# A fused adaLN attention and MLP kernel: the turn of x's blocks 1 to 3 moved from TensorE to VectorE and DRAM, with new instruction orders

## The chip, the cores and the metric

One core of a Trainium2 chip runs the whole kernel. The metric is the device time of one execution in microseconds; less is better. Inputs and outputs are fp32 in DRAM.

The engines are called TensorE (PE in the profile, PEld for its weight loads), VectorE (DVE), ScalarE (ACT), GpSimd (POOL) and SyncE (SP). SP issues nearly all DMAs here.

## The reference

One block of a transformer with adaptive layer norms: linear attention, then an MLP with SiLU. S = 2048 tokens, D = 576, H = 32 heads of 18, F = 4608.

```
mod = silu(c) @ w_mod                      # (1,576) @ (576, 6*576)
sa, ca, ga, sb, cb, gb = six rows of mod
h = layernorm(x) * (1 + ca) + sa
q, k, v = heads of h @ wqkv                # (2048,576) @ (576,1728)
pq, pk = phi(q), phi(k)                    # t+1 where t > 0, else exp(t); + 1e-6
kv = sum over tokens of pk^T v             # per head, 18 x 18
z  = sum over tokens of pk
x = x + ga * (((pq @ kv) / (pq . z)) @ wo)
h = layernorm(x) * (1 + cb) + sb
out = x + gb * (silu(h @ w1) @ w2)
```

## The kernel before

**Number format.** Products run in fp32r, a format that TensorE takes in one pass. Each fp32 operand is split in a high part (a cast on ACT, `split_h` L205, `w_hi` L309) and a low part (a subtraction on VectorE or GpSimd, `sub_hi` L121, `w_lo` L315 and L317). A product is hi·hi + hi·lo + lo·hi. The contraction over D = 576 goes in four chunks of 128 (KC = 4) and a tail of 64, whose high and low part share the 128 rows. So one output bank takes 14 matmuls (`x_passes` L222): per chunk hi·hi, hi·lo, lo·hi, in chunk order 0 to 4.

**Tokens.** 16 tiles of 128 (NT), in 4 blocks of 512 (NB). `hT[tb]` holds a block's normalised, modulated x with D on the partitions, in high and low parts.

**Stages.** First the head (to about 37 us): the modulation columns of the first layer norm come from w_mod, the tiles of block 0 are turned by TensorE (`turn_tiles` L387), and k and v of tiles 0 and 1 are computed. Then a loop over the tiles t = 0 to 15 (from L643): k projection, v projection, the products kv of tile t−1 (`kv_mm`), and q projections of the first eight tiles (`q_proj`, q0 and q1 at t = 1). wq for the q projections is loaded into rooms of `acc` and split at t = 1 (`split_w`). At t = 4 and t = 7 two thirds of w_mod's rest are multiplied by silu(c) (`mod_piece` L508), of which the first piece is loaded (`raw`, L266) and scaled (`tmod`, L517) much earlier by the written order. After the loop come the attention output, the second layer norm and the MLP, whose h streams through DRAM and whose main units (L1324 and on) run from 372 us to the end. From about 400 us on code and order stay as they are.

**The turn of blocks 1 to 3 in before.** At t = 0, 4, 8 `load_x` (L258) loads the four tiles of the next block into `xt` (a pool with four places). At i = t mod 4 = 1 the statistics, and the normalised rows in place: tiles 1 and 3 on ACT (L191), 0 and 2 on VectorE (L193). At i = 2 and 3 `turn` (L633) takes one chunk after the other: four TensorE transposes of 128x128 into the PSUM bank psT (`transpose_chunk` L212 to L214), then on ACT the modulation out of PSUM (L199) and the cast to the high part (L205), then on VectorE the low part. That makes 3 blocks x 5 chunks x 4 = 60 transposes. The next block is first used by the k projection at the next t = 4, 8, 12.

**Order.** ORDERS holds for each engine a list of instruction numbers; `arrange` ties each instruction behind the one before it in the list. In before TensorE's list changes two places only, since the program's own order holds there (`manual_schedule`); VectorE, ACT, GpSimd and SP have long lists up to about 400 us.

**Rooms.** A tile of a pool waits until the users of the tile whose place it takes are done. `xt_133` and `xt_135` (136 and 138 in before) are x's tiles 2 and 3; the third and fourth tile of block 1 take their places.

Of the kernel before, what the change touches and what calls it, by code (L numbers as in the profile page):

```python
# [16 lines left out]
P = 128  # L17
# [5 lines left out]
def kernel(ctx: ExitStack, tc, A_x, A_wqkv, A_wo, B_x, B_w1, B_w2, c, w_mod, out):  # L23
# [28 lines left out]
    def f32(ap):  # L52
# [4 lines left out]
            0-106 114 107-109 115 110-113 116-2586  # L57
        """,
        "DVE": """
            0 3 2 1 4 6-7 11 8 12-13 9-10 14-16 18 17 5 19-22 30 23-24 28-29 25-27 43 31 44 33-34 36 35 37-38 32 39  # L60
            41 40 42 45-47 50 48-49 62-63 51-53 57 84 64 55 58 65 59 86 66 85 87 60 56 80 67 88 81 83 68 82 69 71 70
            72 122 73-74 61 89 54 75 78 76 90 77 79 123 91 124 92-93 96-97 125 98 94 126-127 100 99 95 101 103-104
            107 105 108 106 109 111 102 132-133 135 110 134 136 138-139 137 140-144 112 145 148 113 146 149 147 114
            117 115 118 116 119-121 128-129 131 150-151 225 223 130 226 224 222 152-155 157-158 156 159 162 176 160
            177-178 161 179-181 163 165 228 227 166-167 164 169-170 168 171-173 193-197 199 198 200 202 201 203-205
            174 209 206-207 210 208 175 182 185 183 186 188 187 184 189-190 192 191 211-213 216 214 217 215 218 220
            219 221 229 232 230 233 231 234-237 240 238-239 241-243 246 244 247 245 248-249 252 250-251 253-256 258
            257 259 263 260-262 266 268 267 270 269 271 264-265 272-273 275-277 274 281 279 282 278 280 283-284 288
            285 289 286 295-296 290 306 303 302 291 307 292 314 293 315 294 297 323 304 298-299 324 308 331 287 300
            309 301 310-311 305 312 316 332 340 313 317-319 341 320-321 325 351 322 326-329 352 362 330 333-336 338  # L70
            363 337 339 344 370 345-347 342-343 349 348 353 371 380 354-359 350 360 381 361 398 364-369 399 416
            372-375 377 376 378 417 424 385 382 384 379 387-388 391-392 394 425 402 386 389 403 390 404-407 393 383
# [568 lines left out]
    with tc.manual_schedule(engines={mybir.EngineType.PE}):  # L641
        for t in range(NT):
# [4 lines left out]
            if t > 1:  # L647
                k_proj(t)
# [944 lines left out]
```

## Time and profile before

| what | us |
|---|---|
| median of three timed runs (1137.52 to 1138.51) | 1137.76 |
| profiled execution, span from its first to its last instruction | 1136.9 |
| time around the span (the median less the span) | 0.9 |
| TensorE busy in the span | 1126.8 |
| VectorE busy | 971.0 |
| GpSimd busy | 649.3 |
| ACT busy | 538.7 |

In a row of the timeline the first number is the start, the second the time from the first start to the last end of so many equal instructions. TensorE's matmuls overlap, so the spacing of starts tells what one costs. In a row of the windows stand the length, the busy times of PE, PEld, DVE, ACT and POOL with their counts, then the granted clock, the share of the DMA engines' time and GB/s. A row of the waits names who waited at which line, for whom, the sum in us, the count and the longest.

### The profile page before, as it was taken

How to read it: one execution, taken by the hardware profiler on the slowest of the kernel's cores; microseconds unless marked ns; L12 is line 12 of the kernel's file. 1: busy time of each engine (PE TensorE's matmuls, PEld its weight loads, DVE VectorE, ACT ScalarE, POOL GpSimd, SP SyncE). 2: the span in 40 equal slices, each digit the busy share in tenths (PEclk: the TensorE clock that was granted, in tenths of full speed). 3: DMA queues.
4: the chain of work that ended last, by engine and by line, in shares of the span. 5: the costliest groups of instructions: out<-in, count | busy, mean ns of one | idle time of the engine just before them, and what ended most of it. 6: DMA issues, size and time to landing. Idle time of an engine off the chain costs nothing.

```text
span 1136.9 us, 19287 instructions
## 1 busy us (share of the span) xinstructions
PE 1126.8 (99%) x7033; PEld 1040.8 (92%) x7033; DVE 971.0 (85%) x1543; ACT 538.7 (47%) x1112; POOL 649.3 (57%) x743
## 2 busy tenths in 40 slices
PE   8999999999999999999999999999999999999998
PEld 7999999999998899999999999999989999999998
DVE  6866744686878899999999999999999999999996
ACT  5643442547556544445445444444444444444441
POOL 1100000374714777767775776677667767776786
PEclk9999999999999999999999999999999999999999
DMA  9621100223359877976978869779778697697684
GB/s 281 199 84 31 44 7 1 71 84 116 137 198 354 340 274 256 348 278 257 361 261 315 314 250 356 273 255 364 261 277 331 265 344 281 258 346 274 256 310 156
DMA packets 58813, 269.03 MB, mean 237 GB/s; under 512 B 5724, under 2 KB 21856, under 8 KB 35680
## 3 DMA queue, kind: packets, MB, share of 16 engines
q1 hardware_dynamic: 58708, 267.80, 64.4%
q8 instruction: 56, 0.92, 0.3%
q14 instruction: 37, 0.30, 0.1%
q10 hardware_dynamic: 12, 0.00, 0.0%
HBM read 250.12 MB, written 16.78 MB: 235 GB/s over the span
## 4 chain that ended last, share of the span: by engine, by line
PE 94%; DMA 3%; DVE 1%; ACT 1%; POOL 0%; SPq 0%; issue 0%; POOLq 0%
PE up L1324 34%; PE down L1397 32%; PE psK L226 12%; PE big L226 7%; PE small L886 2%; PE big L897 2%; PE kvp L589 1%; DMA hT<-in_w_mod_dram 1%; PE big L812 1%; DMA raw<-in_w_mod_dram 1%; DMA hT<-hd 1%; PE small L214 1%; DMA xt<-in_A_x_dram 1%; PE up L1427 1%; PE down L1427 1%; PE psT L214 1%
## 5 line engine op out<-in xcount | busy, mean ns | idle before, releaser
L1405 DVE TENSOR_TENSOR acc<-down,acc 128x576 f32<-128x576 f32 x330 | 246.2, 754 | 13.2 <-PE down L1397 3.2
L1324 PE MATMUL up<-hT,w 128*128 128x512 f32 x916 | 239.4, 390 | 0.5 <-DMA hT<-hd 0.5
L1324 PEld LDWEIGHTS up<-hT,w 128*128 128x128 f32 x916 | 164.5, 188 | 25.4 <-DMA hT<-hd 0.7
L1359 POOL TENSOR_TENSOR s<-f,f 128x256 f32<-128x256 f32 x66 | 52.3, 792 | 159.7 <-ACT f L1340 159.7
L1397 PE MATMUL down<-w,hb 128*128 128x288 f32 x792 | 120.6, 294 | 0.0
L1397 PE MATMUL down<-w,hc 128*128 128x288 f32 x792 | 120.6, 294 | 0.0
L1397 PEld LDWEIGHTS down<-w,hc 128*128 128x128 f32 x792 | 113.7, 188 | 5.4 <-PE up L1324 0.3
L1397 PEld LDWEIGHTS down<-w,hb 128*128 128x128 f32 x792 | 113.7, 188 | 5.3
L121 DVE TENSOR_TENSOR w<-v,w 128x288 fp32r<-128x288 f32 (+1 forms) x170 | 114.8, 684 | 2.8 <-ACT w L1058 2.8
L1405 DVE TENSOR_TENSOR U<-down,U 128x576 f32<-128x576 f32 x132 | 99.6, 754 | 17.1 <-PE down L1397 15.2
L226 PE MATMUL psK<-w,hT 128*128 128x352 f32 (+3 forms) x506 | 106.4, 336 | 1.1 <-POOL w L317 0.6
L1324 PE MATMUL up<-room,w 128*128 128x512 f32 x348 | 91.0, 390 | 0.0
L1378 POOL TENSOR_TENSOR hc<-s,hc 128x512 fp32r<-128x512 f32 x66 | 89.4, 1355 | 0.1
L184 POOL TENSOR_TENSOR rstd<-ve,neghalf 128x4 f32<-128x4 f32 (+3 forms) x10 | 9.5, 953 | 138.8 <-DVE ve L183 138.8
L226 PEld LDWEIGHTS psK<-w,hT 128*128 128x128 f32 x506 | 81.8, 188 | 7.5 <-POOL w L317 0.8
L1340 ACT ACTIVATE f<-f 128x512 f32<-128x512 f32 x102 | 64.5, 632 | 47.8 <-DVE f L1345 24.8
L1343 DVE TENSOR_TENSOR f<-up,p 128x512 f32<-128x512 f32 x102 | 69.7, 683 | 12.1 <-PE up L1324 11.2
L1066 ACT CAST w<-v 128x288 fp32r<-128x288 f32 x85 | 36.7, 434 | 76.4 <-PE down L1397 62.1
L1324 PEld LDWEIGHTS up<-room,w 128*128 128x128 f32 x348 | 62.5, 188 | 9.4
L1363 POOL TENSOR_TENSOR f<-f,s 128x256 f32<-128x256 f32 x66 | 51.2, 776 | 34.9 <-DVE hb L1378 24.5
L1397 PE MATMUL down<-w,he 128*128 128x288 f32 x396 | 63.0, 294 | 0.0
L1397 PE MATMUL down<-w,ha 128*128 128x288 f32 x396 | 63.0, 294 | 0.0
(310 smaller groups left out, 2529.7 us busy)
## 6 DMA issues: line engine op xcount, KB each, us to landing
hT<-hd SPq DMA_DIRECT2D x66, 1280.0 KB, 5.5
hT<-hd SPq DMA_DIRECT2D x45, 1024.0 KB, 5.5
room<-hd SPq DMA_DIRECT2D x35, 1280.0 KB, 5.7
room<-hd SPq DMA_DIRECT2D x20, 1024.0 KB, 5.1
v<-in_B_w_dram SPq DMA_DIRECT2D x17, 576.0 KB, 7.2
v<-in_B_w_dram SPq DMA_DIRECT2D x17, 512.0 KB, 7.1
hd<-S SPq DMA_DIRECT2D x6, 1024.0 KB, 3.8
xt<-in_A_x_dram SPq DMA_DIRECT2D x16, 288.0 KB, 5.2
```

Source lines behind the costliest of these rows:

```text
L121: return V.tensor_sub(lo, full, f32(hi))
L214: T.transpose(ps[:, i * P : (i + 1) * P], xt[i][:, cidx * P : (cidx + 1) * P], ident)
L226: T.matmul(ps, xpart(a), wpart(b), start=n == 0, stop=n == len(XW) - 1)
L1066: A.copy(self.w2[n][:, 0], src)
L1324: T.matmul(ps, left, right, start=first and m == 0, stop=m == len(seq) - 1, skip_group_check=True)
L1340: A.activation(self.f[i, k], self.f[i, k], AF.Silu)
L1343: V.tensor_add(f, self.bank[bank[1]], self.p1)
L1359: G.tensor_add(self.s[:, 0:1], half(i, 0, 1), half(i, 1, 1))
L1363: G.tensor_sub(half(i, 1, 0), half(i, 1, 0), self.s[:, 1:2])
L1378: eng.tensor_sub(t[:, :, 1, :], src, f32(t[:, :, 0, :]))
L1397: T.matmul(ps[:, p, :HALF], self.a[i, n][:, u, p * P : (p + 1) * P], self.w.w2[n][:, v], start=n in (1, 5, 7, 6) and j == 0, stop=j == 2, ...
L1405: V.tensor_add(dst, ps[:, :, :HALF], dst)
```

## The change

- `load_x`: in blocks 1 to 3 tile i holds the rows 128a + 32i to 128a + 32i + 31 of the block, for a = 0 to 3, in its partitions 32a and up. Four transfers of 32x576 load it instead of one of 128x576.
- `normalise` leaves out the doubled last 64 columns there, and in block 1 all four tiles are normalised on ACT.
- `turn_squares`: four VectorE transposes, one for each tile, each turning a tile's 32x32 squares in place of one another, into `squares` (a part of `acc` not yet used); four stores write them to DRAM in runs of 128 numbers, so that the DRAM tile holds the block with D as rows.
- `turn`: `load_turned` reads a chunk of 128 rows x 512 tokens back (the last chunk of 64 rows twice, in two halves), and ACT modulates in SBUF instead of out of PSUM.
- `mod_col`: the moving operand `ones` is 32 columns wide instead of 128.
- The split of wq stands before the statistics of block 1 at t = 1; `load_wo` comes at t = 12 instead of 10, since `acc`'s rooms are used until then.
- `manual_schedule` is left out, and ORDERS has new lists for all engines: some 2527 TensorE instructions, up to about 400 us, are placed one by one. Two further paths in the diff (`SQUARES`) are not taken, the tuple being empty.

```diff
     def normalise(self, i, xt, r, eng, tail=True):
-            for o, lo, hi in ((D, KC * P, D), (0, 0, D)):
+            for o, lo, hi in ((D, KC * P, D), (0, 0, D))[not tail :]:
...
     def load_x(tb, i):
-        nc.sync.dma_start(xt[:, :D], x[(tb * 4 + i) * P : (tb * 4 + i + 1) * P, :])
+        if tb == 0:
+            nc.sync.dma_start(xt[:, :D], x[i * P : (i + 1) * P, :])
+        else:
+            for a in range(4):
+                r0 = tb * 512 + a * P + 32 * i
+                nc.sync.dma_start(xt[32 * a : 32 * a + 32, :D], x[r0 : r0 + 32, :])
...
     def mod_col(col, a, t):
-        ps = ps2().rearrange("p a b -> p (a b)")
+        ps = ps2()[:, 0, : (KC + 1) * 32].rearrange("p (k q) -> p k q", q=32)
         for k in range(KC + 1):
-            T.matmul(ps[:, k * P : (k + 1) * P], t[:, k * P : (k + 1) * P], ones, start=True, stop=True)
+            T.matmul(ps[:, k], t[:, k * P : (k + 1) * P], ones[:, :32], start=True, stop=True)
...
+    free = acca[:, QB : NT, :].rearrange("p t d -> p (t d)")
+    squares = free[:, : 4 * D].rearrange("p (b i j) -> p b i j", i=4, j=32)
+    places = [free[:, (KC + 1 + n) * 512 :][:, :512] for n in range(4)]
+    xd = [dram.tile([D, 512], F32, name=f"xd{n}") for n in range(1 + NB)]
+
+    def turn_squares(xts):
+        for i in range(4):
+            V.transpose(squares[:, :, i, :], xts[i][:, :D].rearrange("p (b j) -> p b j", j=32))
+        for a in range(4):
+            rows = slice(32 * a, 32 * a + 32)
+            nc.sync.dma_start(xd[NB][:, a * P : a * P + P].rearrange("(b j) t -> j b t", j=32),
+                              squares[rows].rearrange("j b i t -> j b (i t)"))
+
+    def load_turned(dst, src, k):
+        if k < KC:
+            nc.sync.dma_start(dst, src[k * P : (k + 1) * P, :])
+        else:
+            for h in range(2):
+                nc.sync.dma_start(dst[h * 64 : h * 64 + 64], src[KC * P : D, :])
+
     def turn(tb, k):
-        ps = psT()
-        transpose_chunk(xts, k, ps)
-        h32 = pa.tile([P, 512], F32, name="h32")
-        modulate_split(ps, k, hT[tb], cols["a"], h32)
+        h32 = places[CHUNKS.index(k)] if k != 3 else pa.tile([P, 512], F32, name="h32")
+        load_turned(h32, xd[NB], k)
+        modulate_split(h32, k, hT[tb], cols["a"], h32)
...
+            if t == 1:
+                for k in START:
+                    split_w(wqp_, k, acc[10 + k], V)
             if more and i == 1:
...
-                    ln.normalise(j, xts[j], xts[j], A if j % 2 else V)
+                    ln.normalise(j, xts[j], xts[j], A if tb == 0 or j % 2 else V, False)
+                turn_squares(xts)
...
-            if t == 10:
+            if t == 12:
                 load_wo()
```

Three places of the new order follow, all at tile 1, in before and after the change. First SP, from the last pieces of wq (`acc` from wqkv) to the last tile of block 1; `raw_972` (now `raw_974`) is the first piece of w_mod's rest, `xt_398` and `xt_400` (now `xt_401` and `xt_406`) are the third and fourth tile of block 1. Before:

```order
L260 DMA xt_394<-in_A_x_dram 128x576
L230 DMA acc2_97<-in_A_wqkv_dram 128x576
L230 DMA acc3_98<-in_A_wqkv_dram 128x576
L230 DMA acc2_97<-in_A_wqkv_dram 128x576
L230 DMA acc3_98<-in_A_wqkv_dram 128x576
L260 DMA xt_396<-in_A_x_dram 128x576
L266 DMA raw_972<-in_w_mod_dram 128x1152
L260 DMA xt_398<-in_A_x_dram 128x576
L260 DMA xt_400<-in_A_x_dram 128x576
```

And now:

```order
L311 DMA acc_95<-in_A_wqkv_dram 128x576 x2
L313 DMA acc_95<-in_A_wqkv_dram 64x576
L311 DMA acc_95<-in_A_wqkv_dram 128x576
L346 DMA xt_401<-in_A_x_dram 32x576
L352 DMA raw_974<-in_w_mod_dram 128x1152
L346 DMA xt_401<-in_A_x_dram 32x576
L311 DMA acc_95<-in_A_wqkv_dram 128x576
L346 DMA xt_401<-in_A_x_dram 32x576 x2
L346 DMA xt_406<-in_A_x_dram 32x576 x4
L352 DMA raw_977<-in_w_mod_dram 128x1152
```

The load of raw and one piece of wq, which stood ahead of the third tile's load, now stand behind the first of its four transfers.

Second VectorE, around the last low parts of wq (`wq_107`, now `wq_104`; L315 and L317, now L401 and L403); `vx` are the parts of v, `hT` those of block 0, `tmod` is the scaled raw. Before:

```order
L121 TENSOR_TENSOR vx1_153<-psK_491,vx1_153 128x2x126
L179 BN_AGGR mv_459<-st_467 128x2
L317 TENSOR_TENSOR wq_107<-acc3_98,wq_107 64x576
L121 TENSOR_TENSOR vx1_153<-psK_491,vx1_153 128x2x126
L121 TENSOR_TENSOR hT_102<-raw_156,hT_102 128x256
L178 BN_STATS st_471<-xt_398 128x6
L121 TENSOR_TENSOR vx1_153<-psK_491,vx1_153 128x72
L178 BN_STATS st_471<-xt_398 128x6
L178 BN_STATS st_475<-xt_400 128x6
L179 BN_AGGR mv_459<-st_471 128x2
L178 BN_STATS st_475<-xt_400 128x6
L517 TENSOR_SCALAR tmod_971<-raw_972,sc_87 128x2x576
```

And now:

```order
L201 TENSOR_TENSOR vx0_149<-psK_422,vx0_149 128x2x126
L401 TENSOR_TENSOR wq_104<-acc_95,wq_104 128x576
L201 TENSOR_TENSOR vx0_149<-psK_422,vx0_149 128x72
L603 TENSOR_SCALAR tmod_973<-raw_974,sc_87 128x2x576
L401 TENSOR_TENSOR wq_104<-acc_95,wq_104 128x576
L201 TENSOR_TENSOR vx1_150<-psK_514,vx1_150 128x2x126
L201 TENSOR_TENSOR hT_99<-raw_152,hT_99 128x256 x2
L201 TENSOR_TENSOR vx1_150<-psK_514,vx1_150 128x2x126
L401 TENSOR_TENSOR wq_104<-acc_95,wq_104 128x576
L201 TENSOR_TENSOR vx1_150<-psK_514,vx1_150 128x72
L403 TENSOR_TENSOR wq_104<-acc_95,wq_104 64x576
```

tmod stood behind all of wq's low parts; now three of these stand behind it, the first of them that of chunk 1.

Third TensorE, at the end of v1 (`psK_491`, now `psK_514`) and the beginning of q0 (`psK_552`, now `psK_565`). Before, where the transpose of xt_136 stands one row above:

```order
L390 MATMUL psT_526<-ident_85,xt_138 128x128
L589 MATMUL kvp0_108<-pk0_150,vx0_152 128x256
L589 MATMUL kvp0_108<-pk0_150,vx0_152 128x128
L589 MATMUL kvp0_108<-pk0_150,vx0_152 128x256
L589 MATMUL kvp0_108<-pk0_150,vx0_152 128x128
L589 MATMUL kvp1_109<-pk0_150,vx0_152 128x256
L589 MATMUL kvp1_109<-pk0_150,vx0_152 128x128
L589 MATMUL kvp1_109<-pk0_150,vx0_152 128x256
L589 MATMUL kvp1_109<-pk0_150,vx0_152 128x128
L589 MATMUL kvp2_110<-pk0_150,vx0_152 128x256
L589 MATMUL kvp2_110<-pk0_150,vx0_152 128x128
L226 MATMUL psK_552<-wq_107,hT_102 128x288 x28
```

And now:

```order
L476 MATMUL psT_549<-ident_85,xt_133 128x128
L307 MATMUL psK_514<-w_103,hT_99 128x256
L307 MATMUL psK_514<-w_103,hT_99 128x324
L307 MATMUL psK_514<-w_103,hT_99 128x256
L307 MATMUL psK_565<-wq_104,hT_99 128x288
L307 MATMUL psK_514<-w_103,hT_99 128x324
L476 MATMUL psT_549<-ident_85,xt_135 128x128
L307 MATMUL psK_565<-wq_104,hT_99 128x288 x12
L676 MATMUL kvp0_105<-pk0_147,vx0_149 128x128
```

The last transposes of tiles 2 and 3 now lie inside v1, q0's first matmul too, and the ten kv products between v1 and q0 have moved behind q0's first thirteen matmuls.

More of the change, by code (lines that the diff above doesn't have):

```diff
@@ L144 @@
     z = const.tile([P, D], F32, name="z")
-    accb = [accp.tile([P, 4, D], F32, name=f"acc{b}") for b in range(NB)]
-    acc = [accb[t // 4][:, t % 4, :] for t in range(NT)]
+    acca = accp.tile([P, NT, D], F32, name="acc")
+    accb = [acca[:, 4 * b : 4 * b + 4] for b in range(NB)]
+    acc = [acca[:, t, :] for t in range(NT)]
     ones = pa.tile([P, P], F32, name="ones")
@@ L537 @@
     NP0 = 2
+    QB = NT // 2
     def xsel(t):
@@ L1547 @@
     units = [(g, p) for g in range(1, NG) for p in range(2)]
-    with tc.manual_schedule(engines={mybir.EngineType.PE}):
+    with nullcontext():
         fetch(5)
```

194 lines of the change are left out of this document (141 added, 53 removed).

## The prediction

> **What bounds the kernel now.** I read the page first: the span, the busy times and the slices.
>
> ```profile
> span 1136.9 us, 19287 instructions
> PE 1126.8 (99%) x7033; PEld 1040.8 (92%) x7033; DVE 971.0 (85%) x1543; ACT 538.7 (47%) x1112; POOL 649.3 (57%) x743
> PE   8999999999999999999999999999999999999998
> PEclk9999999999999999999999999999999999999999
> ```
>
> TensorE is busy 99% of the span, at an undisturbed clock. So a saving counts if it takes work off TensorE, and a cost counts if it makes TensorE wait. What matters next is where TensorE has time to lose. The table of windows, columns PE, PEld, DVE, ACT and POOL, gives the first 80 us, and in its last row the sum over the 22 windows from 0 to 440 us, in which all instructions lie that the new order places.
>
> ```profile
> 0.00:20.00 20.00, 18.21 (x123) 17.03 (x124) 12.41 (x34) 9.03 (x17) 4.07 (x13) 1.00 0.91 276
> 20.00:40.00 20.00, 17.32 (x127) 16.25 (x126) 16.95 (x39) 18.19 (x40) 4.34 (x3) 1.00 0.68 204
> 40.00:60.00 20.00, 19.52 (x136) 18.65 (x135) 18.24 (x36) 8.47 (x17) 1.05 (x1) 1.00 0.80 235
> 60.00:80.00 20.00, 20.00 (x132) 18.95 (x132) 13.66 (x33) 9.75 (x19) 1.01 (x1) 1.00 0.25 86
> sum 440.00, PE 433.54 PEld 407.20 DVE 322.06 ACT 225.11 POOL 151.44; mean PE 19.71 PEld 18.51 DVE 14.64 ACT 10.23 POOL 6.88
> ```
>
> TensorE idles 6.5 us in these 440, and 4.5 of them lie before 40 us, where ACT (18.19 of 20) and VectorE (16.95) are nearly full. The list of TensorE's waits agrees: no single wait is over 1.3 us.
>
> ```profile
> PE psK L407 <- ACT hT L205: 1.3, 1, 1.3
> PE kvp L412 <- DVE ones L415: 1.1, 1, 1.1
> PE psT L390 <- ACT xt L191: 0.7, 1, 0.7
> PE psK L226 <- POOL w L317: 0.6, 1, 0.6
> PE psK L226 <- DVE acc L333: 0.5, 1, 0.5
> PE psK L777 <- ACT acc L330: 0.4, 2, 0.2
> ```
>
> So there is next to nothing to win from waits after 40 us, and much to lose if a new order puts one in.
>
> **The transposes that go.** Blocks 1 to 3 take 60 transposes, four at a time; the timeline shows one group, in front of the first matmuls of a v projection.
>
> ```profile
> L214 PE MATMUL psT<-ident,xt 128*128 128x128 f32 x60 | 9.0, 272 | 0.0
> 103.16 0.60 PE L214 MATMUL psT<-ident,xt 128*128 128x128 f32 x4
> 103.51 0.48 PE L226 MATMUL psK<-w,hT 128*128 128x512 f32 x1
> 103.83 0.40 PE L226 MATMUL psK<-v,hT 128*128 128x512 f32 x1
> 104.06 1.78 PE L226 MATMUL psK<-w,hT 128*128 128x512 f32 x7
> ```
>
> The group's 9.0 us counts overlapping pipelines. What it costs is the spacing of starts: from 103.16 to 103.83 four transposes and one wide matmul take 0.67 us; the next wide matmul takes 0.23 (103.83 to 104.06); 0.44 remain for four, 0.11 each. Sixty are **−6.5 us** on TensorE. The Trainium skill ("TensorE: Matmul & The Clock Gate", section "Back-to-back issue gap") gives about 81 ns for a sustained matmul of 128 columns; by that, an estimate, the term would be 4.9 us and the forecast below 1.6 us later. The measured 0.11 decides.
>
> **Narrower column matmuls.** mod_col's moving operand shrinks from 128 columns to 32.
>
> ```profile
> 107.26 1.28 PE L526 MATMUL psK<-ones,tmod 128*128 128x128 f32 x10
> 108.30 1.35 PE L589 MATMUL kvp<-pk,vx 128*128 128x256 f32 x10
> 9.78 1.10 PE L371 MATMUL kvp<-ones,hT 128*128 128x64 f32 x8
> 10.72 1.06 PE L371 MATMUL kvp<-sc,hT 128*128 128x64 f32 x8
> ```
>
> Ten passes of 128 columns start 1.04 us apart from what follows (107.26 to 108.30), 0.104 each; eight of 64 columns take 0.94 (9.78 to 10.72), 0.118 each. Width does not set the spacing here, so the two calls give **0**, at most 0.3.
>
> **The first q projection (the term I trust least to be nothing).** The order of SP, VectorE and TensorE at the end of tile 1 is new, as the rows under the change show. Three instructions now stand in a line that did not before. On SP the first transfer of xt_401 waits until TensorE has read xt_133, whose place it takes; that is near the end of v1. The load of raw_974, and the last big piece of wq's load, stand behind it on SP. On VectorE the instruction that reads raw_974 (tmod) stands ahead of a subtraction that makes wq's low part of chunk 1. TensorE needs this low part at the ninth matmul of q0 (psK_565), and only 13 instructions lie between the last transpose of xt_133 and that matmul. The prices:
>
> ```profile
> 36.81 0.70 PE L226 MATMUL psK<-w,hT 128*128 128x256 f32 x4
> 37.35 0.38 PE L390 MATMUL psT<-ident,xt 128*128 128x128 f32 x2
> 38.67 7.66 PE L226 MATMUL psK<-wq,hT 128*128 128x288 f32 x56
> 46.17 0.46 PE L226 MATMUL psK<-w,hT 128*128 128x352 f32 x2
> 27.73 0.36 SPq L266 DMA_DIRECT2D raw<-in_w_mod_dram  x1
> raw<-in_w_mod_dram SPq DMA_DIRECT2D x1, 576.0 KB, 3.9
> 42.70 0.80 DVE L517 TENSOR_SCALAR tmod<-raw,sc 128x1152 f32<-128x1152 f32 x1
> 35.99 0.75 DVE L315 TENSOR_TENSOR wq<-acc,wq 128x576 fp32r<-128x576 f32 x1
> ```
>
> q matmuls start 7.50 / 56 = 0.134 us apart (38.67 to 46.17), so the 13 take 1.75 us. The chain takes 0.3 for the transpose to drain, 0.36 for the issue, 3.9 to land, 0.80 for tmod and 0.75 for the subtraction: 6.1 us. TensorE waits 6.1 − 1.75 = 4.35. Behind this, the last wq chunk lands later and two subtractions of 0.75 stand in front of its own, which I put at 0.6. The bank that q0 fills is emptied by VectorE behind the statistics of the four tiles, and k2 waits for it; before loses 0.5 for the same thing (the row behind L333), so I add nothing. Sum 4.95, taken as **+5.0**, bounds 3.5 (the transfer of raw_974 lands in 3.0, as x's below do, and the 0.6 is covered) and 6. In before raw_972 was issued at 27.73 and read at 42.70, behind all of wq, so nothing hung on it. Deeper in the chain everything shifts alike.
>
> **The head.** Its instructions are the same in kind, in new order. Before loses 4.5 us there; the new order puts the same transposes between matmuls one by one. I take **−0.4**, bounds −1.5 and +1.0 from the waits listed above (1.3 and 1.1 are the largest single ones that could go or be doubled).
>
> **The way through DRAM.** For blocks 1 to 3 the normalised rows are turned in squares by VectorE, stored by four DMAs in runs of 512 B, read back by six, and modulated in SBUF; ACT's two operations and VectorE's subtraction per chunk stay. This work is off TensorE, so its price is nothing as long as the chunks are ready when k4 begins. The rows, in before's clock:
>
> ```profile
> 45.40 0.15 DVE L185 SCALAR_TENSOR_TENSOR nm<-mv,rstd 128x4 f32<-128x4 f32 x1
> 27.33 0.85 ACT L191 ACTIVATE xt<-xt,nm,rstd 128x576 f32<-128x576 f32 x1
> q1 hardware_dynamic: 3880, 5.49, 90.9%
> hd<-S SPq DMA_DIRECT2D x6, 1024.0 KB, 3.8
> xt<-in_A_x_dram SPq DMA_DIRECT2D x4, 288.0 KB, 3.0
> 51.12 0.78 ACT L199 ACTIVATE h<-psT,col_a 128x512 f32<-128x512 f32 x1
> 51.92 0.62 ACT L205 CAST hT<-h 128x512 fp32r<-128x512 f32 x1
> 73.60 0.45 PE L226 MATMUL psK<-w,hT 128*128 128x352 f32 x2
> ```
>
> The factors are ready at 45.55. Four normalisations on ACT, 0.85 each between other work, end near 50; the fourth VectorE transpose (no row shows one; a 128x576 operation takes 0.75 in the row of wq above, and I take that) near 52, VectorE being 91% busy there. The stores are 2304 packets of 512 B. 3880 packets took 16 engines × 20 us × 0.909 (third row), 75 ns each on an engine, so 2304 take 10.8 us at most; a store of 1 MB of long runs took 3.8. They land between 56 and 63. Loads of this size take 3.0: 59 to 66. Each chunk takes ACT 0.78 + 0.62 = 1.4, so the first is ready at 60 to 68 and the fifth at 66 to 73. k4 begins at 73.60 in before; with block 1's 20 transposes gone (2.2 us) at 71.4, and its last chunk is used some 3.6 us later. So it is hidden by 3 us at the slow end. For blocks 2 and 3 the distance is the same three tiles. I take **+0.3** with ends 0 and +8 (the rival below).
>
> **Later waits.** Of the 6.5 us that TensorE idles up to 440 us, 2.0 lie after 40 us and 1.5 after 60 (the windows above). With all engines ordered anew up to 400 us about half of these may go: **−0.7**, ends −1.5 and +1.5. SP carries 36 more transfers of x and 30 of the turned blocks; at the 0.36 us of the row above that is 24 us in 400, which SP has. Vector and ACT work is moved, not added, beyond twelve transposes of 0.75, 9 us of a VectorE that TensorE's waits do not name after 52 us.
>
> The sum: −6.5 + 0 + 5.0 − 0.4 + 0.3 − 0.7 = −2.3 us against an execution of 1137.8 (span 1136.9 and 0.9 around it, the median of the runs being 1137.76): **1135.5 us**.
>
> **The rivals.**
> - *Full gain*, 0.22: raw_974 is in place in time, because TensorE itself reaches v1's end later than VectorE's queue, or the transfer lands in 2 us. For it: the head's waits may push TensorE, not the loads. Against it: the chain is tied to TensorE's own transpose, so it moves with it. It gives −6.5 − 0.4 + 0.3 − 0.7 = −7.3, **1130.5**.
> - *Slower, the stores are the bound*, 0.15: four stores with rows of 512 B and an element order turned between the two sides take not 4 to 11 us but 18. Then block 1's first chunk comes at 52 + 18 + 3 + 1.4 = 74.4, 3.0 later than k4 wants it, and blocks 2 and 3 lose half as much each: 1135.5 + 6 = **1141.5**. From 15 us per set of stores on it costs anything (52 + 15 + 4.4 = 71.4), and from 17.3 on it makes the kernel slower by more than 0.2% (2.3 + 1.15 + 1.15 = 4.6 us on top of the forecast). For it: the windows show DMA 80% busy between 40 and 60. Against it: 25% after 60. The Trainium skill ("VectorE: DVE Perf Modes", section "The three transpose paths") warns that a plain strided DMA copy used as a transpose is 19 times slower than the transposing path when the innermost stride at the destination is large. Here the innermost runs are contiguous, and no run shown has such a transfer.
> - *Finer interleaving costs*, 0.13: up to 400 us the products of TensorE now alternate singly between banks and stages, and small waits for ACT and VectorE of the size seen above (0.2 to 0.5) come back some eight times, 2.5 us: **1138.0**.
> - The forecast itself, 0.50, own range 1133.5 to 1138.
>
> **How the numbers follow.** A measurement of this kernel tells about 0.2%, 2.3 us, from no change: faster is below 1135.5, slower above 1140.0. The forecast's half lies about evenly on the two sides of 1135.5 (0.25 and 0.24, 0.01 slower); the full gain is faster (0.22); the late stores are 0.13 slower and 0.02 same; fine waits 0.10 same and 0.03 slower. That makes faster 0.47, same 0.36, slower 0.17. The range goes from 1129.0 (full gain with the head's best end is 1129.4) to 1141.0, which leaves out the worse half of the late stores.
>
> **What would show it.** Right: no L214 on psT before 200 us; one TensorE wait of 3 to 5 us in the first q projection, with VectorE's tmod waiting for raw at that time; k4 beginning without a wait; TensorE's busy sum to 440 us lower by about 6.5. Wrong: k4, k8 or k12 waiting for hT behind DMA (the stores), no wait in q0 (full gain), or many short waits in place of one.

## The result, and the profile after

The changed kernel takes 1148.93 us (median of six runs, 1147.51 to 1150.55) against 1138.13 for the kernel before: a ratio of 1.0084, 95% interval 1.0064 to 1.0105. It is slower by 9.6 us by the ratio, 10.8 between the medians. The profiled execution took 1149.6 us with a span of 1147.5. The page's first rows:

```profile
span 1147.5 us, 19282 instructions
PE 1126.8 (98%) x6973; PEld 1038.9 (91%) x6973; DVE 979.3 (85%) x1547; ACT 538.1 (47%) x1108; POOL 646.9 (56%) x743
PEclk9899999999999999999999999999999999999999
```

Sixty matmuls are gone (7033 to 6973), yet TensorE's busy time is to the tenth what it was. So two things happened: TensorE idles 20.7 us of the span where it idled 10.1, and the sixty transposes' time has been eaten by something that makes other matmuls longer. The windows of 20 us show where, with the sum over the first 440 us last.

```profile
0.00:20.00 20.00, 14.64 (x89) 13.82 (x90) 9.09 (x28) 4.75 (x9) 4.06 (x11) 0.91 0.90 285
20.00:40.00 20.00, 17.66 (x121) 16.81 (x120) 16.97 (x36) 16.69 (x33) 4.45 (x5) 0.91 0.40 122
40.00:60.00 20.00, 15.41 (x100) 15.12 (x99) 12.90 (x29) 9.09 (x21) 1.04 (x1) 0.83 0.59 167
60.00:80.00 20.00, 20.00 (x130) 18.70 (x129) 19.12 (x37) 8.73 (x16) 1.01 (x1) 1.00 0.74 193
sum 440.00, PE 423.34 PEld 396.35 DVE 322.07 ACT 220.57 POOL 141.16; mean PE 19.24 PEld 18.02 DVE 14.64 ACT 10.03 POOL 6.42
```

Idle time of TensorE, after less before: 5.36 − 1.79 = +3.6 in the first 20 us, −0.3 in the next, 4.59 − 0.48 = +4.1 from 40 to 60, nothing from 60 to 80, and 4.4 − 1.5 = +2.9 in the other 360. That is the 10.2 by which the sums differ. And the granted clock, 1.00 in all these windows of before, is 0.91, 0.91 and 0.83. Some windows of 2 us (same columns):

```profile
34.00:36.00 2.00, 2.00 (x11) 1.98 (x10) 2.00 (x7) 1.14 (x3) 1.13 (x3) 0.55 0.00 0
46.00:48.00 2.00, 0.00 (x0) 0.00 (x0) 0.97 (x2) 0.00 (x0) 0.00 (x0) 0.51 1.06 299
48.00:50.00 2.00, 1.43 (x6) 1.43 (x7) 1.12 (x3) 1.40 (x4) 0.00 (x0) 0.50 0.80 163
50.00:52.00 2.00, 2.00 (x11) 2.00 (x11) 1.97 (x6) 1.10 (x4) 0.00 (x0) 0.50 0.77 244
```

For some microseconds the clock is at half. What the 20-us windows lack in clock is (0.09 + 0.09 + 0.17) x 20 = 7.0 us; about 1.3 of that fell on an idle TensorE (1.0 in the second of these rows, 0.3 in the third). So slow matmuls took back some 5.7 us, about what the transposes had cost. The six executions differ by this clock as well: their spans are 1147.5 to 1148.5 us at a mean clock of 0.994, and 1145.4 to 1146.1 at 0.996 or 0.997. Each stretch follows a wait of TensorE, which the list of its waits names:

```profile
PE psK L307 <- DVE wq L401: 4.6, 1, 4.6
PE psT L476 <- DVE xt L274: 2.2, 1, 2.2
PE psK L307 <- DVE acc L419: 1.6, 1, 1.6
PE psK L307 <- DVE a L419: 1.6, 1, 1.6
```

In before the longest was 1.3. Four new waits stand ahead of everything. The first is the one in q0 that the prediction describes; the timeline gives its chain, first TensorE (the square bracket says how long it waited, and for whom), then SP, then VectorE.

```profile
42.80 1.18 PE L307 MATMUL psK<-wq,hT 128*128 128x288 f32 x7
48.57 1.57 PE L307 MATMUL psK<-wq,hT 128*128 128x288 f32 x5 [4.59 <-DVE wq L401]
```

```profile
42.30 0.33 SPq L346 DMA_DIRECT2D xt<-in_A_x_dram  x1
42.72 0.37 SPq L352 DMA_DIRECT2D raw<-in_w_mod_dram  x1
...
43.62 0.41 SPq L311 DMA_DIRECT2D acc<-in_A_wqkv_dram  x1
```

```profile
47.03 0.82 DVE L603 TENSOR_SCALAR tmod<-raw,sc 128x1152 f32<-128x1152 f32 x1 [5.47 <-DMA raw<-in_w_mod_dram]
47.77 0.75 DVE L401 TENSOR_TENSOR wq<-acc,wq 128x576 fp32r<-128x576 f32 x1
```

SP's first load of xt_401 is released at 42.30, by the transpose at 42.00; raw is issued behind it at 42.72 and read at 47.03; the low part of wq follows at 47.77, and TensorE goes on at 48.57. VectorE stood still for 5.5 us ahead of work that was ready.

The turn itself, the new operations, is on time. VectorE's transposes and the DMAs of the turn:

```profile
L728 DVE STREAM_TRANSPOSE acc<-xt 128x576 f32<-128x576 f32 x12 | 8.8, 760 | 0.9 <-ACT xt L272 0.9
xd<-acc SPq DMA_DIRECT2D x12, 288.0 KB, 4.4
acc<-xd SPq DMA_DIRECT2D x9, 256.0 KB, 4.5
```

A transpose takes 0.76 us, a store lands after 4.4, a load after 4.5, and TensorE has no wait for hT at k4, k8 or k12.

### The profile page after: what moved, and what is told of

Same layout as the page of the kernel before. It is cut to its first block, busy times and chain, and to the rows that moved or that the text cites. A ratio compares the mean times of both kernels' runs of the same rounds, so it can differ in the third digit from the quotient of the medians.

```text
span 1147.5 us, 19282 instructions
## 1 busy us (share of the span) xinstructions
PE 1126.8 (98%) x6973; PEld 1038.9 (91%) x6973; DVE 979.3 (85%) x1547; ACT 538.1 (47%) x1108; POOL 646.9 (56%) x743
## 4 chain that ended last, share of the span: by engine, by line
PE 92%; DMA 3%; DVE 2%; ACT 2%; SPq 1%; issue 1%; POOL 0%; DVEq 0%; POOLq 0%; ACTq 0%
PE up L1443 33%; PE down L1516 31%; PE psK L307 12%; PE big L307 6%; PE big L1005 2%; PE small L994 1%; PE kvp L676 1%; DMA raw<-in_w_mod_dram 1%; PE big L920 1%; DMA hT<-hd 1%; PE small L295 1%; PE kvp L498 1%; PE up L1546 1%; PE down L1546 1%; DMA v<-in_B_w_dram 0%
## 5 line engine op out<-in xcount | busy, mean ns | idle before, releaser
L1443 PE MATMUL up<-hT,w 128*128 128x512 f32 x916 | 242.7, 390 | 0.6 <-DMA hT<-hd 0.3
L307 PE MATMUL psK<-w,hT 128*128 128x512 f32 (+3 forms) x506 | 117.2, 342 | 3.2 <-DVE acc L419 1.6
L1462 DVE TENSOR_TENSOR f<-up,p 128x512 f32<-128x512 f32 x102 | 69.5, 682 | 11.7 <-PE up L1443 10.2
L307 PE MATMUL big<-w,qT 128*128 128x288 f32 x352 | 70.8, 308 | 0.2 <-DVE acc L934 0.2
L307 PE MATMUL psK<-wq,hT 128*128 128x288 f32 x336 | 58.9, 305 | 5.4 <-DVE wq L401 4.6
```

The source lines that it names most:

```text
L307: T.matmul(ps, xpart(a), wpart(b), start=n == 0, stop=n == len(XW) - 1)
L1443: T.matmul(ps, left, right, start=first and m == 0, stop=m == len(seq) - 1, skip_group_check=True)
L1462: V.tensor_add(f, self.bank[bank[1]], self.p1)
```

## The experiments

Theory at the start: the loss is in the places of a few instructions in the queues of SP and VectorE, plus the half clock behind the waits; the turn costs nothing. Rivals: the half clock is the main price; or the turn has a price of its own on VectorE and the DMA engines. The kernels of one group below ran on the same chip, and each ratio is to the kernel before on that chip.

| run | median us | ratio, 95% interval |
|---|---|---|
| the changed kernel | 1148.93 | 1.0084 [1.0064, 1.0105] |
| busy_wait | 1149.01 | 1.0080 [1.0058, 1.0102] |
| sp_order | 1142.70 | 1.0031 [1.0020, 1.0042] |
| dve_order | 1150.51 | 1.0089 [1.0062, 1.0116] |
| head_of_before | 1138.52 | 0.9995 [0.9982, 1.0007] |
| order_of_before | 1141.07 | 1.0021 [1.0007, 1.0035] |
| ends_of_before | 1137.30 | 0.9993 [0.9977, 1.0010] |
| busy_head | 1143.97 | 1.0058 [1.0038, 1.0077] |
| narrow_cols | 1138.02 | 1.0003 [0.9989, 1.0016] |
| turn_placed | 1143.39 | 1.0038 [1.0026, 1.0050] |
| ends_q7 | 1134.50 | 0.9957 [0.9942, 0.9973] |
| three_moves | 1142.49 | 1.0032 [1.0021, 1.0043] |
| queues_placed | 1142.65 | 1.0028 [1.0016, 1.0039] |
| z_behind | 1139.21 | 0.9999 [0.9983, 1.0014] |
| squares_free | 1143.52 | 1.0042 [1.0025, 1.0059] |

In the diffs, numbers are places in the lists of ORDERS.

### First group: the wait in q0

**sp_order.** SP's list: the last big piece of wq (29) and the load of raw_974 (73) go ahead of xt_401's first transfer (42).

```diff
-26 30 27 42 73 40 29 41 39
+26 30 27 29 73 42 40 41 39
```

> The changed kernel with two numbers of SP's list moved: the last piece of wq and raw_974 ahead of the first transfer of xt_401 (as in before). VectorE's list stays. Theory (SP's queue is what makes q0 wait): the wait of 4.6 us goes and the 2.2 us of half clock behind it with it, 6.8 us less, about 1142. Rival (VectorE's list is the cause, or the loads are slow wherever they stand): the wait stays over 2 us, 1146 or more.

Measured: the wait of 4.6 is gone; 40 to 60 us is as full as before, and at full clock:

```profile
40.00:60.00 20.00, 19.43 (x139) 18.77 (x138) 18.77 (x36) 10.06 (x21) 1.04 (x1) 1.00 0.69 191
```

From 1.0084 to 1.0031 is 0.53%, 6.0 us, which by the two intervals can be 2.6 less or more: the wait of 4.6, and some of the half clock. The two traces don't part these, since the profiled sp_order also kept its clock at 32 us (0.91 from 20 to 40 us in the changed kernel, 1.00 here) with nothing moved there. Two places in SP's queue are the largest part of the loss.

**dve_order.** The other end of the same line: on VectorE, tmod (122) moves behind wq's last low part (66).

```diff
-58 62 59 122 63 85 60 56 86 65 87 66 73
+58 62 59 63 85 60 56 86 65 87 66 122 73
```

> The changed kernel with one number of VectorE's list moved: tmod behind the last low part of wq (as in before). SP's list stays. Theory: the low part of chunk 1 no longer waits for raw_974, but the last piece of wq still stands behind xt_401 on SP, is there some 3 us after its issue at 43.6 and needs 1.4 us more of ACT and VectorE, so q0 waits about 2.5 us at its fourth chunk in place of 4.6 and the half clock stays: about 1146.5. Rival (VectorE's list alone was the cause): the same 6.8 us less as the other run, 1142.

Measured: nothing gained, a miss. TensorE now waits twice in q0:

```profile
PE psK L321 <- ACT wq L409: 3.4, 1, 3.4
PE psK L321 <- DVE wq L415: 1.9, 1, 1.9
```

ACT's cast of wq waits for wq's own piece, which on SP still stands behind xt_401's load. So the cause is SP's queue; VectorE's order was the second in line.

**busy_wait.** Eighteen fp32 matmuls of ones into an unused bank fill q0's wait (x in TensorE's list), which keeps the clock up.

```diff
+            if t == 1:
+                warm_up(18, kvp[2][:, 1])
...
-191-202 181 188
+191-197 x 198-202 181 188
```

> The changed kernel, and ahead of the ninth matmul of q0, where TensorE waits 4.6 us, 18 matmuls of ones into an unused part of a PSUM bank (their result is read by nobody; the rest is as it was). Theory (a wait is paid twice: after it TensorE runs at half clock for some microseconds; the windows from 48 to 54 us lose 0.7 + 1.0 + 0.4 = 2.2 us so): the wait stays, its idle time is filled, the clock stays full, about 2.2 us less than the changed kernel's 1148.9, that is 1146.7. Rival (the rows after the wait are slow for another cause, such as DMA traffic or matmuls that alternate between banks): 1148.9, with the same low clock in the windows.

Measured: the clock is 1.00 behind the wait, and the time is as it was. The two intervals together leave 3 us either way, so the times alone can't tell the 2.2 expected from nothing; the trace can. From q0's first matmul to a run of twenty q matmuls, which begins at 63.73 in the changed kernel and at 62.49 here, it takes 20.9 us instead of 21.2. So about 0.4 is gained. TensorE reaches the same operands sooner and waits for them (the row sums two waits, 0.95 and 0.61):

```profile
PE psK L324 <- DVE wq L418: 1.6, 2, 0.9
```

So the half clock in q0 is mostly no price of its own: VectorE and ACT are late too, and slow matmuls fill the time until they have caught up. As the main price of the whole loss that rival falls; in the head the half clock does cost something (busy_head and z_behind below).

**head_of_before.** All five lists as in before up to the end of q1, the new order from there; first rows of TensorE's list:

```diff
-            37 0 38 1 39-40 2 41 3-5 8 42 6 51-52 7 9-10 19-20 11 21 12-13 29-30 14 31 15 22 16-17 32 18
+            0-106 114 107-109 115 110-113 116-277 296 278-280 288 298-317 281 318-325 282 297 283-284 289
```

> The changed kernel's code, with all five lists in before's order up to the end of q1 (46 us in before) and in the new order from there on. Theory (the loss lies in the order of the first 60 us, some 11 us of it by the traces): about 1138. Rival 1 (the way through DRAM and its stores slow the kernel): 1147 to 1149, since the turn is as it was. Rival 2 (matmuls placed one by one cost something everywhere): a part only, 1143 or more.

Measured as expected, 0.9995. From sp_order's 1.0031 the rest of the first 45 us makes 0.36%, 4.1 us. So the net loss lies in the first 55 us, and behind them the turn just pays for what its new order costs.

### Second group: the turn in before's order

**order_of_before.** All lists as in before; only the turn's operations are put in, in order of their times. TensorE's list is the program's own order again.

```diff
-            37 0 38 1 39-40 2 41 3-5 8 42 6 51-52 7 9-10 19-20 11 21 12-13 29-30 14 31 15 22 16-17 32 18
+            0-106 114 107-109 115 110-113 116-2526
```

> The changed kernel's code (turn by VectorE and through DRAM, dealt rows, narrow columns), but all five lists as in before, with TensorE in the program's order: the new instructions stand where before's clock lets their data be there (block 1's modulations from 61 us on in place of 51, wo's loads behind block 3). Theory (the new turn takes 6.5 us off TensorE and costs nothing itself; all of the loss is the new order's): 6 to 7 us below before, about 1132. Rival (the turn itself has a price, by VectorE's twelve transposes, ACT's waits of 7.6 us in all for the loads, or 66 more transfers on SP): 1135 to 1139.

Measured: slower than before, a miss for the theory, and above the 1135 to 1139 of the rival too. VectorE, 91% busy here in before, has block 1's transposes ahead of the instruction (L343) that empties q1's bank, and TensorE waits for that bank:

```profile
46.68 2.30 DVE L652 STREAM_TRANSPOSE acc<-xt 128x576 f32<-128x576 f32 x3 [0.27 <-ACT xt L196]
...
51.49 0.75 DVE L343 TENSOR_SCALAR acc<-psK 128x576 f32<-128x576 f32 x1
```

```profile
52.30 0.50 PE L231 MATMUL psK<-w,hT 128*128 128x512 f32 x1 [2.60 <-DVE acc L343]
```

**ends_of_before.** Before's order up to the end of q1 and again behind the loop over the tiles; the new order only between. Against head_of_before only the lists' later parts change, as in VectorE's last row:

```diff
-518 520-521 526 525 532 527 524 528-530 535 523 534 536-539 531 533
+517 516 522 532 523 520-521 527 524-526 528-530 535 534 537 536 538-539
```

> As head_of_before (before's order up to the end of q1), and before's order again for all that the program has behind the loop over the tiles (from 199 us on in before); only the loop's rest is in the new order. Theory (between 260 and 420 us the new order loses some 2.3 us against before's, as the profile of head_of_before shows): 2.3 less than head_of_before, about 1136. Rival (what is lost there comes from what the loop leaves behind, or from the DMA traffic): as head_of_before, 1138.5.

Measured 0.9993, within the scatter of head_of_before's 0.9995; its median is 1.2 us lower, on another chip's run. By the ratios the two are 0.2 us apart, give or take 2.4, so the 2.3 us expected from the order behind the loop did not show, and a smaller gain can't be told from none.

**busy_head.** sp_order with matmuls of ones ahead of the first transpose of x (10), and at the beginning of v0 (7), to keep the clock up in the head. The second fill was meant for the wait ahead of v0's first matmul; in the kernel's list (y) it stands six matmuls later, so that this wait is not filled.

```diff
+        fill("x", 10, kvp[1][:, 0])
...
+        fill("y", 7, kvp[2][:, 1])
...
-118 112 119-121 113 122-123 114
+118 112 119-121 113 y 122-123 114
```

> The run sp_order with two of TensorE's waits in the head filled by matmuls of ones into unused PSUM (10 ahead of the first transpose of x, where it waits 2.2 to 2.8 us, and 7 ahead of v0's first matmul, where it waits 1.6). Theory (the clock is lowered after these waits, and TensorE is what is late behind them): clock 1.00 from 12 to 17 and from 32 to 36 us, up to 3 us less than sp_order's 1142.7, about 1140. Rival (as at q0, what TensorE needs next is late anyway, so the clock matters little): within 1 us of sp_order, though the clock is full.

Measured 1.0058, slower than sp_order's 1.0031, but not a test of the theory. The first fill did what it should: the clock is 1.00 up to 20 us, and from x's first transpose to v0's first matmul it takes 18.8 us (12.31 to 31.13) where sp_order, at half clock for a part of it, takes 20.4 (12.31 to 32.76). The second fill stands behind the wait:

```profile
20.00:40.00 20.00, 17.66 (x123) 17.02 (x123) 15.38 (x34) 15.80 (x31) 4.45 (x5) 0.91 0.57 172
31.13 0.54 PE L330 MATMUL psK<-w,hT 128*128 128x256 f32 x1 [1.62 <-DVE a L442]
32.70 2.65 PE L521 MATMUL kvp<-ones 128*128 128x128 f32 x14
```

The wait of 1.62 is still there, the clock falls to 0.50 after it, and the fill runs into that, in front of v0's other matmuls, for 2.4 us (32.70 to 35.10). So the full clock brought 1.6 us in the head, and the misplaced fill spent more than that.

**narrow_cols.** Before, with mod_col's operand 32 columns wide, that part of the change alone.

```diff
-            T.matmul(ps[:, k * P : (k + 1) * P], t[:, k * P : (k + 1) * P], ones, start=True, stop=True)
+            T.matmul(ps[:, k], t[:, k * P : (k + 1) * P], ones[:, :32], start=True, stop=True)
```

> The kernel before, with mod_col's moving operand 32 columns wide instead of 128 and nothing else changed. Theory (the spacing of such matmuls does not depend on the width): as before, within 0.3 us of it. Rival (narrow matmuls are issued faster): 0.6 us less, which the times can hardly tell but the spacing of the ten matmuls in the profile can.

Measured: no difference beyond the interval, which is 1.5 us either way; the spacing decides. In its timeline the ten passes of one call (five fp32 matmuls, each shown as two) start 1.04 us ahead of what follows, as wide ones did in before:

```profile
106.86 1.20 PE L526 MATMUL psK<-ones,tmod 128*128 128x32 f32 x10
107.90 1.35 PE L589 MATMUL kvp<-pk,vx 128*128 128x256 f32 x10
```

### Third group: single moves

**ends_q7.** ends_of_before, and on VectorE the emptying of a bank of q7's tile (176) goes ahead of the last tmod (182), which waits for raw.

```diff
-180 181 170 182 176 177
+180 181 170 176 182 177
```

> ends_of_before with one VectorE instruction moved: the one that empties a bank of q7's tile (acc<-psK) goes ahead of the last tmod, which waits for raw from DRAM. Theory, the wait of 1.3 us at 130.5 (1.5 lost) is only that queue: 1137.3 - 1.5 = 1135.8. Rival, it is late for another reason as well (ACT, which read the bank 1.1 us before, or the tmod wanted by the column matmuls next): 1137.3, with a wait on tmod or ACT in its place.

Measured 1134.50, ratio 0.9957: faster than both kernels. Its page:

```profile
span 1131.8 us, 19290 instructions
PE 1121.7 (99%) x6973; PEld 1034.2 (91%) x6973; DVE 977.0 (86%) x1547; ACT 537.1 (47%) x1108; POOL 649.9 (57%) x743
PEclk9999999999999999999999999999999999999999
```

TensorE idles 1131.8 − 1121.7 = 10.1 us, just what it idled in before, at full clock, and both its busy time and the span are 5.1 us shorter. This is the saving of the sixty transposes with nothing given back. The wait at 130 us shrank from 1.3 to 0.5 (on tmod, for the column matmuls). That is 0.8 of the 2.8 us between the medians; the rest lies in small waits at places that the move doesn't touch, and since the same move brings nothing in three_moves I can't say that it alone did it.

**three_moves.** sp_order, that move, and on ACT the copy bc_ga (97) ahead of two modulations, the first of which (118) waits for a turned load.

```diff
-180 181 170 182 176 177
+180 181 170 176 182 177
...
-90 91 109 118 114 97 95
+90 91 109 97 118 114 95
```

> The changed kernel with three moves: that of sp_order on SP, that of ends_q7 on VectorE (at 138.7 us), and on ACT the copy bc_ga ahead of the second modulation that waits for block 2's turned load (at 102.2 us). Theory, each of the later waits is one queue's order: 1142.7 - 1.6 - 0.8 = 1140.3. Rival, they are taken over by the next thing in line: 1142.7. Neither touches the head's 4 us, which stay.

Measured 1.0032 against sp_order's 1.0031: a miss. Both waits are gone from the list, and two others of their size stand there, for operands that were hidden behind them:

```profile
PE psK L321 <- DVE vx L215: 1.3, 2, 0.9
PE psK L626 <- DVE tmod L620: 0.5, 1, 0.5
```

**turn_placed.** order_of_before, with the emptying of q1's bank (91; 61 is its exponential on ACT) ahead of the transposes (81 to 84), and v3's last 8 columns (110, 80) ahead of statistics and the last modulation.

```diff
-80 90 81 82 83 84 123 91 124
+80 90 91 81 82 83 84 123 124
...
-109 111 102 132 133 135 110 134
+109 110 111 102 132 133 135 134
```

> The turn through VectorE and DRAM stays, the order is that of order_of_before (before's, with the turn's operations put in), with four instructions moved: on VectorE the instruction that empties q1's bank goes ahead of block 1's four transposes, on ACT its exponential goes ahead of the second of the four normalisations, and the emptying of v3's last 8 columns goes ahead of the last chunk's modulation (ACT) and ahead of block 2's statistics (VectorE). Theory, the turn is free and only the place of its work in VectorE's and ACT's queues costs: the waits of 2.6 at 52.3 us and 1.7 at 76.1 us go, with the half clock behind the first (about 1.4), so 1141.1 - 5.7 = 1135.4; no wait of TensorE over 1 us between 45 and 80 us. Rival, the turn has a price of its own (a fuller VectorE, ACT and DMA queue): other waits of the same size take their place, 1139 to 1141.

Measured 1.0038, a miss. The two waits are gone as expected, and a longer one has come:

```profile
52.32 3.46 SPq L655 DMA_DIRECT2D xd<-acc  x4
55.89 5.10 SPq L276 DMA_DIRECT2D raw<-in_w_mod_dram  x3
```

```profile
63.20 1.41 DVE L529 SCALAR_TENSOR_TENSOR tmod<-raw,sc,tmod 64x1152 f32<-64x1152 f32 x1 [4.10 <-DMA raw<-in_w_mod_dram]
```

```profile
65.09 0.87 PE L231 MATMUL psK<-w,hT 128*128 128x352 f32 x2 [4.46 <-DVE vx L125]
```

The stores wait on SP for VectorE's transposes until 52.3; a load of raw is queued behind them; tmod waits for raw; and the emptying of v2's bank is queued behind tmod. It is the chain of q0 once more, through the new stores.

### Fourth and fifth group: following the wait

**queues_placed.** VectorE empties the banks of k2, v2 and q2 (93, 96, 99, 101) ahead of tmods (124 to 127); SP loads the turned chunks (51 to 56) ahead of two loads of raw (88, 89).

```diff
-50 77 88 89 51-56 90 57
+50 77 51-56 88 89 90 57
```

> turn_placed, in which a wait of 4.5 us at 60.6 us and one of 1.1 at 56.7 came in: a load of raw stood on SP behind the four stores of the turn (issued 52.3 to 55.8, behind VectorE's transposes), landed at 63, and VectorE's last tmod, which needs it, stood ahead of the instruction that empties v2's last 8 columns. Here VectorE empties the banks of k2, v2 and q2 ahead of the tmods of that stretch, and SP issues the loads of the turned chunks ahead of two more loads of raw. The turn itself is unchanged. Theory, the loss was the queues': both waits go, none over 1 us between 40 and 80 us, 1143.4 - 4.5 - 1.1 - 1 (half clock behind them) = 1136.8. Rival, the turn's work has a price of its own that moves from queue to queue: a wait of over 2 us elsewhere before 90 us, 1140 or more.

Measured 1.0028, the rival's number, with the rival's wait. (The profiled execution took 1147.55, 4.9 over the median; a wait of 2.8 us behind 360 us is part of that.) The stretch from 40 to 66 us is at last without loss, and then the next queue is late:

```profile
60.00:70.00 10.00, 8.77 (x56) 8.06 (x56) 6.30 (x11) 7.35 (x12) 0.00 (x0) 1.00 0.97 325
```

```profile
63.57 13.33 SPq L270 DMA_DIRECT2D xt<-in_A_x_dram  x16
```

```profile
78.70 0.82 DVE L183 BATCH_NORM_STATS2 st<-xt 128x6 f32<-128x288 f32 x2 [0.97 <-DMA xt<-in_A_x_dram]
79.87 0.75 DVE L343 TENSOR_SCALAR acc<-psK 128x576 f32<-128x576 f32 x1
```

The DMA engines are 97% busy from 60 to 70 us (18% in the same stretch of before), the loads of x's block 2 go out until 76.9, VectorE's statistics wait for them, and a bank's emptying stands behind the statistics: TensorE waits 4.5 us at 76.

**z_behind.** three_moves, and on VectorE the two copies that make z (9, 10) go behind the first statistics.

```diff
-1 0 9-10 2-3 7 6 11-12 8 13-14 18
+1 0 2-3 7 6 11-12 8 13-14 9-10 18
```

> three_moves with one more move: on VectorE the two copies that make z, which wait for ACT's sc until 6.2 us in the changed kernel and in before stand behind the first layer norm's statistics, go behind these statistics again. Theory, TensorE's wait of 2.2 to 2.6 us at 9.5 us (the first transpose waits for VectorE's normalised xt) is this one place in VectorE's queue, since the statistics start at 6.74 in the changed kernel and at 3.84 before: 1142.5 - 2.4 = 1140.1. Rival, the head's 4 us lie in TensorE's finer order and in later operands (weights, tmod from DRAM): the wait is taken over by these, 1142.5.

Measured 0.9999 against three_moves' 1.0032: 0.33%, 3.8 us (give or take 2.2) for one place in a list, more than the 2.4 expected. VectorE in before, then in the changed kernel, then here:

```profile
3.84 1.19 DVE L178 BATCH_NORM_STATS2 st<-xt 128x6 f32<-128x288 f32 x3 [2.60 <-DMA xt<-in_A_x_dram]
5.62 0.34 DVE L435 COPY z<-sc 64x64 f32<-64x64 f32 x2
```

```profile
6.20 0.39 DVE L521 COPY z<-sc 64x64 f32<-64x64 f32 x2 [4.99 <-ACT sc L516]
6.74 1.54 DVE L259 BATCH_NORM_STATS2 st<-xt 128x6 f32<-128x288 f32 x4
```

```profile
3.72 0.82 DVE L273 BATCH_NORM_STATS2 st<-xt 128x6 f32<-128x288 f32 x2 [2.49 <-DMA xt<-in_A_x_dram]
7.26 0.42 DVE L535 COPY z<-sc 64x64 f32<-64x64 f32 x2
```

The copies held VectorE for 5.0 us, and for about the last half of that x's first tile was there, by the rows of before and of this run. TensorE's first transpose of x, in three_moves and then here:

```profile
12.31 0.30 PE L490 MATMUL psT<-ident,xt 128*128 128x128 f32 x1 [2.56 <-DVE xt L288]
10.25 0.30 PE L490 MATMUL psT<-ident,xt 128*128 128x128 f32 x1 [0.46 <-DVE xt L288]
```

It waits 0.5 instead of 2.6 and starts 2.1 us earlier, and the first 20 us hold 16.72 of TensorE's work instead of 14.64. The clock stays at full speed throughout, and from this transpose to v0's first matmul it takes 18.8 us instead of 20.4, as in busy_head. So the 3.8 us are the wait, 2.1, and the half clock behind it, 1.6.

**squares_free.** queues_placed, with half of block 2's loads (57 to 64) ahead of the turned chunks on SP, the others ahead of raw, and q3's bank (112) ahead of the statistics.

```diff
-50 77 51-56 88-90 57-72
+50 77 57-64 51-56 65-72 88-90
```

> queues_placed, in which the loss moved to a wait of 4.5 us at 76 us: the sixteen loads of x's block 2 stood on SP behind the turned chunks' loads (63.6 to 75.0 us), VectorE's statistics waited for them, and the instruction that empties q3's bank stood behind the statistics. Here the first eight of these loads go ahead of the turned chunks' loads on SP, the other eight ahead of three loads of raw, and the emptying of q3's bank goes ahead of the statistics on VectorE. Theory, only the queues cost and the turn is free: the 5.9 and 3.1 us lost from 60 to 100 us shrink to under 2, 1142.7 - 7.5 = 1135.2. Rival, the 2.3 MB that the turn adds for a block to the DMA engines (97% busy from 60 to 70 us) are the price: k4 or VectorE waits for a load again, 1140 or more.

Measured 1.0042, a miss; the rival's number again. The turned chunks now load from 60.4 instead of 58.6, reach ACT 2 us later, and ACT's modulations stand ahead of the casts that empty tile 3's banks. TensorE waits 3.1 us at 66 and about 3 again at 83.

```profile
PE psK L231 <- DVE vx L125: 6.8, 3, 3.1
```

## Why the prediction was wrong

The forecast was 1135.5, range 1129.0 to 1141.0, with 0.17 on slower. The kernel is at 1148.9, slower than any case named. Step by step:

- **Transposes, −6.5.** They are gone, and worth somewhat less: in ends_q7, with TensorE's idle time and clock as in before, span and busy time fell by 5.1, which is 85 ns each and not 110. Before's own trace says the same: in 12 of the 15 groups of four the next matmul starts 0.35 or 0.36 us after the first transpose, 0.09 each. The 0.44 that I took, from a single group, includes what the first matmul behind the transposes takes longer than the next (0.32 against 0.23). The Trainium skill ("TensorE: Matmul & The Clock Gate", "Back-to-back issue gap") has about 81 ns, by which, an estimate, sixty are 4.9 us; ends_q7 is nearer to that than to my spacing. In the other runs at full clock TensorE's busy time fell by less (4.7 in z_behind, 4.0 in ends_of_before, 3.3 in head_of_before); small gaps added elsewhere could make that difference, and the runs don't part the two.
- **Columns, 0.** Right (narrow_cols).
- **q0, +5.0, bounds 3.5 to 6.** Right in chain and size: raw landed 3.9 us after its issue as taken, TensorE waited 4.59 for the 4.35 worked out, and undoing it is worth 6.0, which is within the scatter of the 5.0. I had not thought of the half clock behind the wait; by busy_wait's trace it adds about 0.4.
- **The head, −0.4, bounds −1.5 and +1.0.** This step failed. I looked at TensorE's list alone, and took the bounds from waits that before has, as if a new order could only shrink or double those. The loss was made on VectorE: the copies of z stand ahead of the statistics, wait for ACT until 6.2 us, and cost 3.8 (z_behind), 1.6 of it by the half clock that follows the wait, for which the sum had no term. The place can be read in the order, and the time at which ACT has made sc (5.3 us) in the trace of before.
- **The way through DRAM, +0.3.** Right for what it priced: the stores land in 4.4 us, inside the 4 to 11, and no k projection waits. Wrong in what it left out. It asked when the chunks are ready, not what stands behind the transposes, stores and loads in their queues. In before's order the kernel is 2.4 to 4.8 us slower than before in all four arrangements tried (order_of_before, turn_placed, queues_placed, squares_free), so that these places cost 7 to 10 with the 5.1 that the transposes give. The four times hardly differ by their intervals, and in the traces the wait that was removed came back one queue further on each time. Of the orders tried only the new one of the loop carries the turn without loss, as ends_q7 shows. Which engine's part of that order does it was not tried.
- **Later waits, −0.7, bounds −1.5 and +1.5.** Failed too. TensorE's idle time after 60 us grew by 2.9. With SP and z mended (z_behind) the kernel is level with before, so the 5 us of the transposes are still lost. The profiled z_behind idles 12.8 us where before idled 10.1, in waits of 1.6 at most, which is about half; where the rest goes stays open. Two such waits were removed in three_moves, and nothing was gained.

The sum with what the runs showed: −5.1 for the transposes, +6.0 for q0, +3.8 for z, and about +5 for the rest of the new order: 9.7 for the 9.6 measured. The last term is what is left over (z_behind is level with before although the transposes are gone), so that the sum closes by construction; the runs show the first three. The rivals were all about the turn and TensorE's interleaving. The slower one (late stores) didn't happen, and none spoke of a queue off TensorE other than q0's.

## What to carry to other kernels

When an order is new on every engine, go through each engine's list for an instruction that waits long (for a load, or another engine's late result) and look at what is ready behind it: that, more than the work moved, set the time here, 6.0 us by two places of SP and 3.8 by one of VectorE. The price of a new step is its place in each queue that it passes, stores and loads included, and a stall that is moved out of one queue is worth something only if nothing behind it is late as well. Undo an order in pieces (the beginning, the middle, the end): that told here where to look, and the middle alone, with one move more, is faster than either kernel.

## What the runs showed of the hardware

- After a wait of TensorE the granted clock fell to about 0.50: for 3.4 us behind 2.2 us (at 11.7), behind 1.62 (at 32.1) and, in order_of_before, behind 2.60; and for 6.8 us, beginning within the wait, at 4.59. It stayed at 1.00 behind 1.62 at 140.9 and behind 1.69 at 76.1 in order_of_before. Even behind the same wait of 1.6 in the head, with the same order up to there, it fell in the changed kernel and in dve_order and stayed at 1.00 in sp_order, busy_wait and three_moves. So the length of the one wait doesn't settle it. The Trainium skill ("TensorE: Matmul & The Clock Gate", "What's actually happening") describes a window of about 3.4 us that runs freely and throttles after an idle one; the stretches of half clock are once or twice that length here, but waits well under one window were enough.
- What the full clock is worth depends on what else is late: 1.6 us from x's first transpose to v0 (18.8 against 20.4 us, busy_head and z_behind), 0.4 us behind the wait in q0 (busy_wait), where VectorE and ACT were late as well.
- VectorE's transpose of 128x576 fp32 in squares of 32 takes 0.76 us, a plain subtraction of that size 0.75: the price assumed for want of a row was right.
- Ten fp32 passes with a moving operand of 32 columns start as far apart as with 128: 0.104 us.
